# Moving runs of exponentials, and the attention steps behind them, inside a fused attention and feed-forward kernel

## The chip, the cores and the metric

The kernel runs on one core of a Trainium2 chip. The metric is the device time of one execution in microseconds (us); smaller is better. The engines that matter here are TensorE (PE in the rows), ScalarE (ACT), VectorE (DVE), GpSimd (POOL) and the queue of SyncE that issues transfers (SP). Each engine takes its own instructions in the order in which the program emits them, and waits at each for what that instruction needs.

## What is computed

An attention with a softmax of q over the head dimension and a softmax of k over the sequence, followed by a feed-forward layer with SiLU:

```python
q, k, v: (batch 8, heads 8, seq 576, head_dim 64)
q_s = softmax(q, axis=-1)                       # exp, row sums, divide
k_s = softmax(k, axis=2)
kv  = einsum('bhsd,bhse->bhde', k_s, v)
x   = einsum('bhsd,bhde->bhse', q_s, kv)        # then (4608 tokens, 512)
h   = x @ w_in                                  # 512 -> 2048
out = (h * sigmoid(h)) @ w_out                  # 2048 -> 512
```

## The kernel before

**Chunks.** The 4608 tokens are worked through in nine chunks t = 0 to 8 (chunk 0 has 576 columns, chunk 1 has 448, the others 512). For each chunk `mm1` (L202) makes 16 blocks of h: four matmuls into one PSUM bank, which ScalarE reads with SiLU into GT (L220). I write mm1(t, i) for the i-th block of chunk t. The second product of chunks 0 and 1 is plain: `mm2` (L324) has 16 steps of four matmuls. Step i = 4 qd + tb works on row block tb and needs the GT blocks 4 qd to 4 qd + 3; the rows for tb = 3 gather in a bank of the PSUM ring. Chunks 2 to 8 use a Strassen form instead: seven products 1, 6, 2, 7, 5, 4, 3 (`product`, L253), each in two halves a and b of eight matmuls of 256 columns, with sums of GT on VectorE before them (`presum`, L227: the S1, S2, S4 of L231, L233 and L237). Products 1 and 2 gather in the same bank A. When 1b is done, ScalarE copies the bank to s1 (L295); product 2 then adds onto that bank, so its first matmul may not start before this copy is done.

**Attention.** Batch b feeds chunk b (576 rows a batch against 512 a chunk, so that batch 7 feeds the last two). Its steps: transfers of q, k, v (L82); four exponentials of 128x1152 on ScalarE, two of q into eq, two of k into ek (L91); sums of eq and their reciprocals on VectorE (L105, L106); the multiplication by these on GpSimd (L111); a cast of v into vaug on GpSimd (L98); one transfer that transposes eq into qT (`tr_dma`, L122, on the SP queue); `kv` on TensorE in two halves (L153) and its scaling on VectorE (`kvcopy`, L165, L166); `xt` on TensorE in two halves (L187) and two copies on ScalarE for each (L198), which give the chunk its XT.

**Tables.** Exponential and SiLU need different tables on ScalarE. So a run of exponentials between SiLUs has a table load ahead of it (in the rows with L91) and one behind it (with L220). Plain copies need none.

**The ring.** Eight PSUM banks: three (`ops`) for the second product, five in a ring for mm1, `kv` (two banks for each half), `xt` (two for each half), and for one row block of mm2 of chunks 0 and 1. A new tile takes the bank of the ring that was given back longest ago in program order, and waits for the last reader of that bank.

**Order.** The program writes a list of units: the mm1 blocks of all chunks in order, and behind chosen mm1 blocks one step of mm2 or one half product (`trail`, L437). From chunk 3 on a chunk has 30 units: mm1(t, 0), (t, 1), (t, 2), then half products and mm1 blocks in turn: 1a, mm1(t, 3), 1b, mm1(t, 4), 6a, mm1(t, 5), 6b, mm1(t, 6), 2a, and so on to 3b; the half products are those of chunk t - 1. The steps of the attention are emitted ahead of a unit that is counted back from the first unit of their chunk (`plan_attn`, L459). A tuple (-34, -34) puts the exponentials of q and of k 34 units ahead; the next ones are for the casts of v, for the transposing transfer, for `kv` and for `xt`. Sums and multiplication of eq stand two and four units behind the exponentials of q, and the loads of the next batch one unit behind the transposing transfer and the casts.

The rest of the order is the same list read from front to back:

```python
    for u, (_, f) in enumerate(units):
        for g in at[u]:
            g()
        f()
```

Of the kernel before, what the change touches and what calls it, by code (L numbers as in the profile page):

```python
# [16 lines left out]
def kernel(  # L17
# [21 lines left out]
    NFB = DFF // 128  # L39
# [37 lines left out]
    def load(b, name, src, ccs=None, eng=nc.sync):  # L77
        if name not in st[b]:
            st[b][name] = ld.tile([128, NG, J * D], FP32, name=name, bufs=LDB[name])
        x = src[b].rearrange("(g r) (p j) d -> g (r p) (j d)", r=2, j=J).rearrange("g x y -> x g y")  # L80
        c = slice(0, NG) if ccs is None else slice(2 * ccs, 2 * ccs + 2)
        eng.dma_start(out=st[b][name][:, c, :], in_=x[:, c, :])  # L82
# [4 lines left out]
    def exp(b, src, dst, cc):  # L87
        if dst not in st[b]:
            st[b][dst] = ap.tile([128, J, NG * D], BF16, name=dst, bufs=1)
        o = st[b][dst][:, :, cc * 128:(cc + 1) * 128].rearrange("p j (g d) -> p j g d", d=D)  # L90
        nc.scalar.activation(out=o, in_=jgd(st[b][src], cc), func=ACT.Exp)  # L91

    def vcast(b, cc, eng):
        o = vaug[b % 2].rearrange("p j (g e) -> p j g e", e=E1)[:, :, 2 * cc:2 * cc + 2, 0:D]
        if eng is nc.scalar:
            eng.copy(out=o, in_=jgd(st[b]["vt"], cc))
        else:
            eng.tensor_copy(o, jgd(st[b]["vt"], cc))  # L98

    def qsum(b, cc):  # L100
        if "zq" not in st[b]:
            st[b]["zq"] = ap.tile([128, 2, J, 2], FP32, name="zq")
            st[b]["rzq"] = ap.tile([128, 2, J, 2], FP32, name="rzq")
        e = st[b]["eq"][:, :, cc * 128:(cc + 1) * 128].rearrange("p j (g d) -> p j g d", d=D)
        nc.vector.reduce_sum(out=st[b]["zq"][:, cc], in_=e, axis=AX.X)  # L105
        nc.vector.reciprocal(out=st[b]["rzq"][:, cc], in_=st[b]["zq"][:, cc])  # L106

    def qnorm(b, cc, eng):
        e = st[b]["eq"][:, :, cc * 128:(cc + 1) * 128].rearrange("p j (g d) -> p j g d", d=D)
        r = st[b]["rzq"][:, cc]  # L110
        eng.tensor_tensor(  # L111
            out=e, in0=e, in1=r[:, :, :, None].to_broadcast([128, J, 2, D]), op=ALU.mult
        )
# [7 lines left out]
    def tr_dma(b, eng):  # L121
        eng.dma_start_transpose(  # L122
            out=qt_tile(b).rearrange("x j c y -> x (j c) y"),
            in_=st[b]["eq"].rearrange("x j y -> x (j y)"),
        )
# [20 lines left out]
    def kv(b, cc):  # L146
        t = [ps.tile([128, 512], FP32, name="kvps", tag="ring", bufs=PSB["ring"]) for _ in range(2)]
        st[b]["kvps", cc] = t
        for j in range(J):
            for g in range(2):  # L150
                for r in range(2):
                    G = 2 * cc + g
                    nc.tensor.matmul(  # L153
                        out=t[r][g * 64:(g + 1) * 64, 0:E1],
                        lhsT=st[b]["ek"][r * P:(r + 1) * P, j, G * D:(G + 1) * D],
                        rhs=vaug[b % 2][r * P:(r + 1) * P, j, G * E1:(G + 1) * E1],
                        start=(j == 0),
                        stop=(j == J - 1),
                    )

    def kvcopy(b, cc):
        for r in range(2):
            kp = st[b]["kvps", cc][r]
            rz = ap.tile([128, 1], FP32, name="rz", bufs=4)
            nc.vector.reciprocal(out=rz, in_=kp[:, D:E1])  # L165
            nc.vector.tensor_scalar_mul(  # L166
                out=kvn[b % 3][:, cc, r, :], in0=kp[:, 0:D], scalar1=rz[:, 0:1]
            )
# [155 lines left out]
    def mm2(t, i):  # L324
        qd, tb = divmod(i, 4)
        if qd == 0:
            tag = "ops" if tb < 3 else "ring"
            OP[t, tb] = ps.tile([128, DM], FP32, name="ops", tag=tag, bufs=PSB[tag])
        n = NFB // 4
        for fc in range(qd * n, (qd + 1) * n):  # L330
            nc.tensor.matmul(  # L331
                out=OP[t, tb],
                lhsT=GT[t][:, fc, tb * 128:(tb + 1) * 128],
                rhs=W2[:, fc, :],
                start=(fc == 0),
                stop=(fc == NFB - 1),
            )
        if qd == 3:
            store(t, tb, tb % 2)

    def store(t, tb, dve=0):
        ost = mp.tile([128, DM], FP32, name="oq", bufs=4)
        if dve:
            nc.vector.tensor_scalar_mul(out=ost, in0=OP[t, tb], scalar1=1.0)
        else:
            nc.scalar.activation(out=ost, in_=OP[t, tb], func=ACT.Copy, scale=1.0)
        for i in range(2):
            b, col = divmod(t * TCH + tb * 128 + i * P, S)
            rows = out[b * S:(b + 1) * S, :].rearrange("(p j) o -> j p o", j=J)[col // P]
            nc.sync.dma_start(out=rows, in_=ost[i * P:(i + 1) * P, :])  # L350
# [86 lines left out]
    def trail(x, key, f):  # L437
        behind[min(max(x, 0), len(xs) - 1)].append((key, f))
# [1 line left out]
    for i in range(NFB):  # L440
        trail(min(5 + i, NFB - 1), ("mm2", 0), lambda i=i: mm2(0, i))
    for i in range(NFB):
        trail(NFB + 5 + i + max(i - 10, 0) * 3 // 2, ("mm2", 1), lambda i=i: mm2(1, i))
    for t in range(STD, NCH):
        for i, (m, a) in enumerate((m, a) for m in ORDER for a in range(2)):
            late = 3 if t == NCH - 2 and i > 6 else 0
# [5 lines left out]
    begin = {t: next(u for u, f in enumerate(units) if f[0] == ("mm1", t)) for t in range(NCH)}  # L452
# [3 lines left out]
    def plan(u, f):  # L456
        at[u].append(f)

    def plan_attn(b, u, sm, vs, tp, ks, ox, eng=nc.gpsimd):  # L459

        for i, (x, y) in enumerate((("qt", "eq"), ("kt", "ek"))):
            plan(u + sm[i], lambda x=x, y=y: [exp(b, x, y, cc) for cc in range(2)])
        for cc in range(2):
            plan(u + sm[0] + 2 + 2 * cc, lambda cc=cc: (qsum(b, cc), qnorm(b, cc, nc.gpsimd)))
            plan(u + vs[cc], lambda cc=cc: vcast(b, cc, eng))
        plan(u + tp, lambda: tr_dma(b, nc.sync))
        if b == 1:
            plan(u + vs[0] + 1, lambda: load_behind(2))  # L470
        elif b + 1 < B:
            plan(u + (tp - 5 if b == 2 else tp + 1), lambda: load(b + 1, "qt", q))
            plan(max(u + tp, u + max(vs)) + 1, lambda: [load(b + 1, *y) for y in (("kt", k), ("vt", v))])
        for cc in range(2):
            plan(u + ks[cc], lambda cc=cc: kv(b, cc))
            plan(u + ks[cc] + 1, lambda cc=cc: kvcopy(b, cc))
        for cc in range(2):
            plan(u + ox[cc], lambda cc=cc: xt(b, cc))

    def load_behind(b):  # L480

        st[b]["qt"] = ld.tile([128, NG, J * D], FP32, name="qt", bufs=LDB["qt"])
        nc.vector.tensor_copy(st[b]["qt"][0:1, 0, 0:1], vaug[(b - 1) % 2][0:1, J - 1, D:E1])
        for x in (("qt", q), ("kt", k), ("vt", v)):
            load(b, *x)

    V = nc.vector
    plan_attn(1, begin[1], (-18, -11), (-6, -5), -11, (-4, -3), (-2, 0), V)
    plan_attn(2, begin[2], (-21, -18), (-14, -13), -13, (-10, -7), (-5, -3))
    plan_attn(3, begin[3], (-25, -20), (-19, -16), -16, (-12, -9), (-6, -4))  # L490
    for b in range(4, B):
        plan_attn(b, begin[b], (-34, -34), (-32, -28), -23, (-14, -10), (-7, -4))
    for cc in range(2):
        plan(begin[NCH - 1] - 7 + 3 * cc, lambda cc=cc: xt(NCH - 1, cc))

# [44 lines left out]
```

## Time and profile before

| | us |
|---|---|
| median of 3 runs | 305.64 (305.04 to 305.79) |
| the profiled execution | 305.13 |
| its span, from the first to the last instruction | 303.3 |
| busy in that span: PE, ACT, DVE, POOL | 272.2, 178.7, 121.0, 53.9 |
| TensorE idle for ScalarE and VectorE, all waits together | 22.5 (the four rows of the group on TensorE's waits) |
| mean granted TensorE clock | 0.98 of full |

A row of a group or of the timeline names the line of the kernel, the engine, the operation, what it writes and reads, and the count; in brackets or behind a bar stands the idle time of the engine just before it and what ended that. Starts are given from the start of the span. Matmuls are pipelined, and the end that a row gives for a matmul is modelled: the next unit starts some 0.17 us before it.

### The profile page before, as it was taken

What the parts mean: (1) busy time and instruction counts of PE and PEld (TensorE: products, weight loads), DVE (VectorE), ACT (ScalarE), POOL (GpSimd) and SP (SyncE); (2) the same over time, 40 slices, a digit from 0 to 9 for tenths busy, and PEclk for the clock granted to TensorE, in tenths of its full rate; (3) what the DMA queues carried; (4) which work ended last, traced back from release to release, by engine and by line L of the source; (5) the groups of instructions that cost most, each with busy time, mean ns of one, the idle gap of its engine ahead of it and who ended that gap; (6) DMA issues with size and microseconds to landing.
All of it is one profiled execution on the core that took longest, in us unless ns stands there. A gap on an engine that the chain in (4) does not pass through costs nothing.

```text
span 303.3 us, 5523 instructions
## 1 busy us (share of the span) xinstructions
PE 272.2 (90%) x2306; PEld 163.3 (54%) x2306; DVE 121.0 (40%) x217; ACT 178.7 (59%) x287; POOL 53.9 (18%) x44
## 2 busy tenths in 40 slices
PE   8799789949789949999799969996999999999993
PEld 3466454414334316665466536654665665666882
DVE  3820425532305252435643474347443241423521
ACT  5694984892996983349744973488335445445110
POOL 0640310080160090002600170008000000000000
PEclk9999999997999968999999999999999999999999
DMA  7999999949149609811595149523212111201144
GB/s 264 270 198 282 325 237 347 317 132 301 53 85 382 219 10 287 284 37 43 107 360 168 46 99 335 198 55 83 47 30 64 37 35 37 69 0 38 40 100 104
DMA packets 42377, 46.43 MB, mean 153 GB/s; under 512 B 18544, under 2 KB 29808, under 8 KB 42352
## 3 DMA queue, kind: packets, MB, share of 16 engines
q1 hardware_dynamic: 37312, 38.35, 42.9%
q0 software_dynamic: 5040, 7.73, 11.5%
q8 instruction: 18, 0.29, 0.4%
q14 instruction: 7, 0.06, 0.1%
HBM read 36.70 MB, written 9.44 MB: 152 GB/s over the span
## 4 chain that ended last, share of the span: by engine, by line
PE 60%; ACT 22%; DMA 8%; DVE 4%; issue 3%; POOL 1%; SPq 0%; ACTq 0%
PE hps L206 27%; PE ops L273 25%; DMA qt<-in_q_dram 6%; ACT ek L91 5%; ACT L220 4%; ACT L91 4%; ACT eq L91 4%; PE ops L331 4%; ACT GT L220 3%; DMA vt<-in_v_dram 3%; DVE SW L231 2%; PE kvps L153 2%; ACT XT L198 2%; PE o L187 2%; DVE SW L233 2%
## 5 line engine op out<-in xcount | busy, mean ns | idle before, releaser
L206 PE MATMUL hps<-XT,W 128*128 128x512 bf16 (+3 forms) x640 | 146.1, 363 | 10.8 <-ACT GT L220 10.2
L220 ACT ACTIVATE GT<-hps 128x512 bf16<-128x512 f32 (+2 forms) x176 | 85.5, 526 | 86.9 <-PE hps L206 86.4
L206 PEld LDWEIGHTS <-W 128*128 128x128 bf16 x640 | 61.6, 99 | 62.0 <-issue 17.4
L273 PEld LDWEIGHTS <-GT 128*128 128x128 bf16 x448 | 43.8, 99 | 21.7 <-ACT GT L220 6.2
L111 POOL TENSOR_TENSOR eq<-eq,rzq 128x1152 bf16<-128x1152 bf16 x14 | 29.8, 2135 | 143.4 <-DVE rzq L106 143.4
L273 PEld LDWEIGHTS <-SW 128*128 128x128 bf16 x336 | 32.6, 98 | 14.5 <-DVE SW L233 3.5
L105 DVE TENSOR_REDUCE zq<-eq 128x18 f32<-128x1152 bf16 x16 | 21.4, 1339 | 41.4 <-ACT eq L91 41.4
L331 PE MATMUL ops<-W,GT 128*128 128x512 bf16 x128 | 33.7, 388 | 4.3 <-ACT GT L220 4.3
L273 PE MATMUL ops<-W,GT 128*128 128x256 bf16 x224 | 30.1, 278 | 5.3 <-ACT GT L220 5.3
L273 PE MATMUL ops<-TW,SW 128*128 128x256 bf16 x224 | 29.2, 273 | 2.7 <-DVE SW L233 2.7
L273 PE MATMUL ops<-TW,GT 128*128 128x256 bf16 x224 | 28.6, 273 | 0.0
L231 DVE TENSOR_TENSOR SW<-GT 128x1024 bf16<-128x1024 bf16 x14 | 14.5, 1032 | 23.9 <-ACT GT L220 23.9
L290 DVE SCALAR_TENSOR_TENSOR u<-ops,s 128x512 f32<-128x512 f32 x14 | 9.7, 692 | 34.9 <-PE ops L273 34.9
L198 ACT CAST XT<-o 128x512 bf16<-128x512 f32 (+3 forms) x36 | 18.3, 564 | 6.4 <-PE o L187 6.4
L331 PEld LDWEIGHTS <-GT 128*128 128x128 bf16 x128 | 12.2, 99 | 16.7 <-ACT GT L220 4.8
L91 ACT ACTIVATE eq<-qt 128x1152 bf16<-128x1152 f32 x16 | 17.8, 1156 | 2.7 <-DMA qt<-in_q_dram 2.6
L91 ACT ACTIVATE ek<-kt 128x1152 bf16<-128x1152 f32 x16 | 17.8, 1152 | 1.6 <-DMA kt<-in_k_dram 1.6
L290 DVE SCALAR_TENSOR_TENSOR oq<-ops,u 128x512 f32<-128x512 f32 x14 | 9.6, 687 | 17.3 <-PE ops L273 14.1
L98 POOL CAST vaug<-vt 128x1152 bf16<-128x1152 f32 x12 | 15.6, 1311 | 0.0
L220 ACT ACT_TABLE_LOAD x11 | 14.1, 1283 | 0.2
L273 PE MATMUL ops<-W,SW 128*128 128x256 bf16 x112 | 14.2, 273 | 0.0
L233 DVE TENSOR_TENSOR SW<-SW,GT 128x1024 bf16<-128x1024 bf16 x14 | 13.0, 930 | 0.5
(45 smaller groups left out, 136.9 us busy)
## 6 DMA issues: line engine op xcount, KB each, us to landing
qt<-in_q_dram SPq DMA_DIRECT2D x6, 1152.0 KB, 6.2
kt<-in_k_dram SPq DMA_DIRECT2D x6, 1152.0 KB, 8.6
vt<-in_v_dram SPq DMA_DIRECT2D x6, 1152.0 KB, 11.7
out_dram<-oq SPq DMA_DIRECT2D x42, 128.0 KB, 2.4
out_dram<-oq SPq DMA_DIRECT2D x60, 64.0 KB, 2.1
W<-in_moe_w_in_dram POOLq DMA_DIRECT2D x4, 512.0 KB, 9.6
W<-in_moe_w_out_dram POOLq DMA_DIRECT2D x4, 512.0 KB, 17.7
qt<-in_q_dram SPq DMA_DIRECT2D x2, 576.0 KB, 4.1
```

What stands on the lines that cost most here:

```text
L91: nc.scalar.activation(out=o, in_=jgd(st[b][src], cc), func=ACT.Exp)
L98: eng.tensor_copy(o, jgd(st[b]["vt"], cc))
L105: nc.vector.reduce_sum(out=st[b]["zq"][:, cc], in_=e, axis=AX.X)
L111: eng.tensor_tensor(out=e, in0=e, in1=r[:, :, :, None].to_broadcast([128, J, 2, D]), op=ALU.mult)
L198: nc.scalar.copy(out=x, in_=o1[g][:, 0:size])
L206: nc.tensor.matmul(out=hps[:, 0:size], lhsT=W1[:, c, fb * 128:(fb + 1) * 128], rhs=XT[t][:, c, off:off + size], start=(c == 0), stop=(c == ...
L220: nc.scalar.activation(out=GT[g][:, fb, col:col + n], in_=hps[:, h], func=ACT.Silu)
L231: V.tensor_add(S1[:, f], quad(t, 0, f, 1), quad(t, 1, f, 1))
L233: V.tensor_sub(S2[:, f], S1[:, f], quad(t, 0, f, 0))
L273: nc.tensor.matmul(out=o[:, a, :], lhsT=l(f), rhs=r(f), start=bool(first and a == 0 and f == 0), stop=(f == HF - 1), skip_group_check=True,)
L290: nc.vector.scalar_tensor_tensor(out=out, in0=o, scalar=1.0, in1=x, op0=ALU.mult, op1=ALU.add)
L331: nc.tensor.matmul(out=OP[t, tb], lhsT=GT[t][:, fc, tb * 128:(tb + 1) * 128], rhs=W2[:, fc, :], start=(fc == 0), stop=(fc == NFB - 1),)
```

## The change

It moves emission points and changes no instruction. The second-product steps of chunk 1 are spread over mm1 blocks 22 to 44 of the whole list (two for every three blocks) in place of blocks 21 to 31 one each and the last five over 33 to 43. The exponentials of batches 4 to 7 move from 34 to 25 units ahead of their chunk, and the steps behind them move later and closer together; batches 2 and 3 get new points of the same kind. Batch 1 and batch 0 stay as they are.

```diff
     for i in range(NFB):
-        trail(NFB + 5 + i + max(i - 10, 0) * 3 // 2, ("mm2", 1), lambda i=i: mm2(1, i))
+        trail(NFB + 6 + i * 3 // 2, ("mm2", 1), lambda i=i: mm2(1, i))
...
     plan_attn(1, begin[1], (-18, -11), (-6, -5), -11, (-4, -3), (-2, 0), V)
-    plan_attn(2, begin[2], (-21, -18), (-14, -13), -13, (-10, -7), (-5, -3))
-    plan_attn(3, begin[3], (-25, -20), (-19, -16), -16, (-12, -9), (-6, -4))
+    plan_attn(2, begin[2], (-16, -10), (-10, -9), -9, (-5, -4), (-3, -1))
+    plan_attn(3, begin[3], (-23, -17), (-17, -15), -15, (-10, -8), (-5, -3))
     for b in range(4, B):
-        plan_attn(b, begin[b], (-34, -34), (-32, -28), -23, (-14, -10), (-7, -4))
+        plan_attn(b, begin[b], (-25, -25), (-23, -21), -14, (-11, -9), (-5, -3))
```

Read off the list of units, the order around the exponentials is this. Before, those of batches 4 to 7 stand ahead of mm1(b-2, 12) for b = 4 and mm1(b-2, 14) for b = 5 to 7, so that the last SiLUs of that chunk come behind them; after, they stand ahead of the half product 1b in chunk b - 1, behind the SiLU of mm1(b-1, 3) and ahead of the copy s1 and the SiLU of mm1(b-1, 4). For batch 2 the exponentials of q stand ahead of mm2(1, 0) in both, with mm1(1, 6) moved in front of them, and those of k move from mm1(1, 7) to mm1(1, 10). For batch 3 they move from mm1(1, 14) and mm1(2, 1) to mm1(2, 1) and mm1(2, 5).

## Rows read from the trace of the kernel before

**Rows 1.** TensorE's waits: for whom, us in total, times, longest us.
```profile
PE hps L206 <- ACT GT L220: 10.2, 5, 4.3
PE ops L273 <- ACT GT L220: 5.3, 3, 1.8
PE ops L331 <- ACT GT L220: 4.3, 1, 4.3
PE ops L273 <- DVE SW L233: 2.7, 3, 0.9
```
**Rows 2.** Timeline of TensorE, chunks 1 and 2: start, us, instruction, [idle before].
```profile
56.11 1.03 PE L331 MATMUL ops<-W,GT 128*128 128x512 bf16 x4
...
60.97 1.03 PE L331 MATMUL ops<-W,GT 128*128 128x512 bf16 x4
...
62.59 0.81 PE L331 MATMUL ops<-W,GT 128*128 128x512 bf16 x3
67.68 0.39 PE L331 MATMUL ops<-W,GT 128*128 128x512 bf16 x1 [4.28 <-ACT GT L220]
...
83.27 2.21 PE L206 MATMUL hps<-XT,W 128*128 128x512 bf16 x8 [1.98 <-ACT GT L220]
...
90.73 1.89 PE L206 MATMUL hps<-XT,W 128*128 128x512 bf16 x8 [0.94 <-ACT GT L220]
92.55 0.48 PE L153 MATMUL kvps<-vaug,ek 64*64 64x65 bf16 x36
92.96 1.04 PE L331 MATMUL ops<-W,GT 128*128 128x512 bf16 x4
...
110.06 3.57 PE L206 MATMUL hps<-XT,W 128*128 128x512 bf16 x8 [4.28 <-ACT GT L220]
113.42 1.91 PE L273 MATMUL ops<-W,GT 128*128 128x256 bf16 x8
```
**Rows 3.** Stretches: us, busy PE, PEld, DVE, ACT, POOL, granted clock, DMA share, GB/s.
```profile
50.00:75.00 25.00, 20.50 (x163) 9.34 (x162) 9.90 (x20) 17.93 (x24) 6.65 (x4) 0.93 0.82 264
75.00:100.00 25.00, 21.96 (x188) 9.49 (x187) 8.26 (x20) 20.68 (x30) 6.39 (x4) 1.00 0.59 188
100.00:110.00 10.00, 5.77 (x33) 2.40 (x32) 3.79 (x5) 9.49 (x12) 3.18 (x3) 0.96 0.37 123
110.00:137.00 27.00, 26.95 (x238) 16.23 (x238) 10.82 (x20) 12.19 (x23) 3.67 (x3) 0.89 0.57 174
137.00:150.00 13.00, 10.33 (x67) 6.29 (x66) 7.88 (x9) 11.78 (x16) 6.85 (x4) 1.00 0.29 63
```
**Rows 4.** Timeline of all engines around the border of chunks 3 and 4.
```profile
137.78 1.28 ACT L91 ACT_TABLE_LOAD   x1
...
139.07 2.22 ACT L91 ACTIVATE eq<-qt 128x1152 bf16<-128x1152 f32 x2
...
141.19 2.20 ACT L91 ACTIVATE ek<-kt 128x1152 bf16<-128x1152 f32 x2
...
142.57 2.41 SPq L320 DMA_DIRECT2D out_dram<-oq  x4
...
144.71 3.05 ACT L220 ACTIVATE GT<-hps 128x512 bf16<-128x512 f32 x6
...
145.36 0.28 PE L273 MATMUL ops<-W,GT 128*128 128x256 bf16 x1 [1.77 <-ACT GT L220]
...
147.44 2.75 SPq L122 DMA_TRANSPOSE qT<-eq  x1
147.58 0.66 ACT L295 ACTIVATE s<-ops 128x512 f32<-128x512 f32 x1
...
149.57 0.61 PE L273 MATMUL ops<-TW,SW 128*128 128x256 bf16 x4 [0.90 <-DVE SW L233]
```
**Rows 5.** The transposing transfers, and a store beside loads (stretch 86 to 93).
```profile
DMA to landing us min/median/max: 4.6/6.2/6.7
out_dram<-oq SPq DMA_DIRECT2D x1, 128.0 KB, 10.3
```

## The prediction

> **What bounds the kernel now.** I read TensorE's waits first. Its rows come to 22.5 us of idle time, and nearly all of it hangs on SiLUs that ScalarE had not done or on sums that waited for such SiLUs [rows 1]. TensorE is therefore the engine whose time counts, and ScalarE sets it back only where it is away for a run of exponentials. The timeline of TensorE gives the places. In chunk 1 it stands still for 4.28 us: the step mm2(1, 4) needs the SiLU of mm1(1, 7), which lies behind both runs of batch 2. In chunk 2 it waits 1.98 and 0.94 us for banks of the ring (batch 3) and then 4.28 us, because the exponentials of batch 4 stand ahead of the SiLU of mm1(2, 12) and all five banks are full [rows 2]. At the next three borders it waits 1.77 us and 0.90 us each: a half product needs the last SiLUs of the chunk, and product 6 the sums made from them [rows 1, 4]. In all 11.48 + 3 x 2.67 = 19.5 us.
>
> The stretches show a second cost. The granted clock is 0.93 in 50 to 75 and 0.96 and 0.89 in 100 to 137 [rows 3]. At half clock that is 25 x 0.07 x 2 = 3.5 us behind the first wait of 4.28 us, and 10 x 0.04 x 2 + 27 x 0.11 x 2 = 6.7 us behind the second, some 0.9 us of which were idle. These cost 1.6 us and 2.9 us of work (half of the busy part of each). Stretches whose longest waits are 1.98 and 1.77 us keep full clock [rows 2 to 4].
>
> **The change part by part.** Nothing is added or removed: the number of runs, and so of table loads, is the same (two for each of batches 1 to 3, one for each later one). What counts is what TensorE can do while ScalarE is away.
>
> *Prices.* One step of mm2 and one mm1 of 448 columns take 62.59 - 60.97 = 1.62 us, split by columns 0.866 and 0.756 us; an mm1 of 512 columns or a half product (8 x 256) costs 0.866 as well [rows 2]. A half of `kv` takes 92.96 - 92.55 = 0.41 us [rows 2], a half of `xt` about as much. A run of four exponentials takes 143.39 - 137.78 = 5.61 us with the load ahead of it, the load behind it 1.3, one of two exponentials 1.29 + 2.2 + 1.3 = 4.8. Waiting SiLUs follow each other every 0.5 us, and s1 takes 0.66 [rows 4].
>
> *Chunks 1 and 2, batches 2 and 3.* I place the new order on the times of before, from 56.11, where mm1(1, 5) has ended. mm1(1, 6) now comes first; its SiLU ends at 57.6 and the exponentials of q hold ScalarE to 62.4. The SiLUs of mm1(1, 7) to (1, 9) end by 63.9, those of k hold it to 68.7, and the SiLU of mm1(1, 10) ends at 69.25. TensorE runs without a wait through mm2(1, 4), to 65.7: that step's GT block is ready at 63.0, so the wait of before is gone. What is late next is the ring. `kv` of batch 2 takes two banks; by the order in which they come free these are those of mm1(1, 9) and mm1(1, 10). It starts at 69.3 and waits 3.55 us. Its second half needs the bank of mm1(1, 13), just issued, and waits 0.8. In chunk 2 the exponentials of q hold ScalarE from 77.3 to 82.2 while four free banks and two mm2 steps cover all but 0.2 us. Those of k hold it from 84.3 to 89.1, and the first half of `kv` of batch 3 waits for the bank of mm1(2, 6), 1.4 us; the ring's next bank then waits some 0.5 us for `kvcopy`, which stands behind the sums S1, S2 on VectorE. Together 6.4 us by starts; a row counts each from the modelled end, 0.17 us later, so 5.5 us in the rows' terms.
> Before, this stretch took 113.42 - 56.11 = 57.3 us, of which 11.5 were waits and 1.6 + 1.6 lost to the clock (of the second low stretch only 110.06 to 113.42 lies in it) [rows 2, 3]; 42.6 us of work remain. After: 42.6 + 5.5 = 48.1. Gain 9.2 us, and 1.3 us for the half clock behind 113.42 that no longer follows: 10.5 us.
>
> *Chunks 3 to 6, batches 4 to 7.* Let T be the start of 1b. The SiLU of mm1(t, 3) ends at T + 0.8, the exponentials at T + 6.4. Behind them on ScalarE stands first s1, then the table load, then the SiLUs. s1 ends at T + 7.1. TensorE does 1b, mm1, 6a, mm1, 6b, mm1, six units, to T + 5.2, and then wants to add product 2 onto bank A, which s1 has not yet read. This wait is new: 1.9 us by starts, 1.75 in the rows' terms, with 2a and all of TensorE's later units queued behind it. The trace of before has no such wait, as s1 there comes early [rows 4]; nearest are the rows of 1.77 and 0.90 us. Its price lies between 0 and 1.9: it is made of single durations, so I take 1.75. The ring isn't the limit: mm1(t, 4) to (t, 8) fill it at about T + 10.6, when SiLUs have run since T + 8.4. At the borders nothing stands ahead of the last SiLUs any more, and S2 has seven units' time to be made, so 2.67 goes. Batch 4: a cost of 1.75 (its old wait is counted above). Batches 5 to 7: 3 x (2.67 - 1.75) = 2.8 gained.
>
> *What moves with them.* Sums, multiplications and casts keep their order among themselves; GpSimd is otherwise empty, VectorE's next due work at the new place is the sum u2, which waits for s1 anyway, and the bank that u2 frees is wanted at T + 10.6. Cover: about 3 us; without it product 7 would wait. The transposing transfer needed 147.44 - 137.78 = 9.7 us from the table load [rows 4], here T + 10.5. On SP it now stands behind the stores of product 2, which wait for their copy behind the caught-up SiLUs (T + 11.1) and issue four times 0.6 us [rows 4]: T + 13.6. It lands 4.6 to 6.7 us later [rows 5], T + 18.2 to 20.3. `xt` wants it twenty units, two `kv` halves and the wait after T: 17.3 + 0.8 + 1.9 = T + 20.0. So it costs 0 to 0.3 us, taken as 0, with no cover left. The loads behind it on SP keep their distance to the next run (18 units); stores of product 5 come behind them as before.
>
> *A rule on table loads.* By the rows, an exponential starts 0.01 us after the end of its table load [rows 4]. [...]
>
> **Sum.** 10.5 - 1.75 + 2.8 = 11.55 us. The profiled execution took 305.13, so 293.6; the median of the runs is 0.5 above it: 294.1.
>
> **The rivals.**
> - *The wait of 3.55 us for the ring costs the clock.* Both waits of 4.28 us did, those up to 1.98 did not [rows 2, 3]; 3.4 in the rows' terms lies nearer the first. Price 1.6 us: 295.7. [...]
> - *s1 doesn't hold product 2.* Then 4 x 1.75 = 7.0 us less, but `xt` comes at T + 18.1 and waits for the transposing transfer, landing up to 1.3 us sooner too as SP is freed sooner; 0 to 2 us of each 1.75 come back: 287 to 294. Against it: product 2 adds onto the very bank that s1 reads.
> - *The four new waits for s1 each cost the clock*, 1.6 us each: 300.5. Against it: 1.77 and 0.90 us at one border cost none [rows 3, 4].
> - *The ring binds more often in chunks 1 and 2* than my placing says, up to 5.5 us again: 294 to 299.6.
> - *Slower: the transposing transfer comes late for `xt`.* From 2.9 us in each of four chunks on ((305.64 - 294.1) / 4) it eats the whole gain, which is a landing 9.3 us after the issue. A store of 128 KB beside the loads took 10.3 [rows 5]; at that, 3.9 us in each: 309.7. Against it: none of the transposing transfers took more than 6.7 [rows 5].
> - *Nothing moves*, since the waits had another cause: 305.6. Against it: each wait's row ends with the SiLU or sum behind the exponentials.
>
> **How the numbers follow.** Forecast 294.1: 0.50 (292.5 to 295.2). Clock lost once: 0.20. s1 doesn't hold: 0.08. s1's waits cost the clock: 0.07. Ring binds more: 0.07. Late transposing transfer: 0.05. Nothing moves: 0.03. A measurement here can tell 0.3%, 0.9 us. Faster 0.92, same 0.03, slower 0.05. The range takes in the first two, the ring and half of the case without s1's wait: 289.5 to 299.5.
>
> **What would show it.** Right: no wait for SiLU at the borders of chunks 3 to 6; a wait of TensorE at L273 for the copy of L295, four times about 1.75 us; a wait of `kv` (L153) for SiLU of 3 to 3.5 us in chunk 1; full clock from 110 on; product 1a of chunk 2 near 104. Wrong: `xt` (L187) waiting for qT, or a clock under 1.00 in chunks 3 to 6. If the first wait is over 4 us, or the four are under 1, my placing of ScalarE's work was wrong.

## The result and the profile after

The changed kernel takes 293.56 us (median of 4 runs, 292.40 to 295.74) against 305.34 us for the kernel before (4 runs): a ratio of 0.9625, 95% interval 0.9558 to 0.9693, or 11.8 us less. A second series of 6 runs on one chip gave 293.39 us against 305.00, the same ratio with the interval 0.9594 to 0.9656. The forecast was 294.1 us, and its range 289.5 to 299.5.

The page of the profiled execution (292.62 us, span 290.7): busy time of TensorE and its clock in 40 slices.

```profile
PE 263.8 (91%) x2269; PEld 162.4 (56%) x2306; DVE 115.7 (40%) x217; ACT 178.0 (61%) x287; POOL 54.9 (19%) x44
...
PEclk9999999999999999999999999999999999999999
```

The two low places of the clock are gone in this execution; another execution of the same kernel shows two others (last experiment). Some matmul records are missing here (2269 of 2306), so the busy time is a little too low. TensorE's waits after the change, to be read against [rows 1] (us in total, times, longest):

```profile
PE ops L273 <- ACT s L295: 6.6, 4, 1.8
PE hps L206 <- ACT GT L220: 3.2, 2, 1.9
PE kvps L153 <- ACT GT L220: 2.8, 3, 1.9
PE kvps L153 <- ACT vaug L96: 2.1, 2, 1.1
PE kvps L153 <- POOL vaug L98: 1.4, 1, 1.4
```

Of [rows 1] only a 3.2 is left, in chunk 0, which the change doesn't touch. Everything at L273 for SiLU or sums and the wait at L331 are gone. New are four waits for s1, 6.6 us, and waits of `kv` of batches 2 and 3 for the ring (2.8) and for GpSimd's cast (1.4). Those for L96 stand in chunk 0, as before. The timeline of TensorE in chunks 1 and 2, against [rows 2]:

```profile
57.95 1.03 PE L331 MATMUL ops<-W,GT 128*128 128x512 bf16 x4
...
65.94 1.03 PE L331 MATMUL ops<-W,GT 128*128 128x512 bf16 x4
68.33 0.19 PE L153 MATMUL kvps<-vaug,ek 64*64 64x65 bf16 x1 [1.37 <-POOL vaug L98]
70.39 0.48 PE L153 MATMUL kvps<-vaug,ek 64*64 64x65 bf16 x35 [1.86 <-ACT GT L220]
70.82 0.92 PE L206 MATMUL hps<-XT,W 128*128 128x448 bf16 x4
71.67 0.48 PE L153 MATMUL kvps<-vaug,ek 64*64 64x65 bf16 x36
...
90.29 0.21 PE L153 MATMUL kvps<-vaug,ek 64*64 64x65 bf16 x1 [0.70 <-ACT GT L220]
90.77 0.48 PE L153 MATMUL kvps<-vaug,ek 64*64 64x65 bf16 x35 [0.27 <-ACT GT L220]
...
104.13 1.04 PE L273 MATMUL ops<-W,GT 128*128 128x256 bf16 x8
```

mm2(1, 4), for which TensorE stood still 4.28 us before, is the row at 65.94 and waits for nothing. `kv` of batch 2 waits 1.37 + 1.86 us instead. Product 1a of chunk 2 starts at 104.13 (113.42 before). The new place of the exponentials, in chunk 3, where the half product 1b starts at 105.86:

```profile
106.68 1.28 ACT L91 ACT_TABLE_LOAD   x1
...
107.97 2.22 ACT L91 ACTIVATE eq<-qt 128x1152 bf16<-128x1152 f32 x2
...
110.09 2.20 ACT L91 ACTIVATE ek<-kt 128x1152 bf16<-128x1152 f32 x2
...
112.20 0.58 ACT L295 ACTIVATE s<-ops 128x512 f32<-128x512 f32 x1
112.79 1.28 ACT L220 ACT_TABLE_LOAD   x1
...
112.83 1.03 PE L273 MATMUL ops<-W,GT 128*128 128x256 bf16 x8 [1.81 <-ACT s L295]
...
119.16 2.77 SPq L122 DMA_TRANSPOSE qT<-eq  x1
```

The copy s1 stands behind four exponentials, and product 2a starts 0.05 us after it has ended. No row of `xt` waits for qT.

### The profile page after: what moved, and what is told of

Same layout as the page of the kernel before. It is cut to its first block, busy times and chain, and to the rows that moved or that the text cites. A ratio compares the mean times of both kernels' runs of the same rounds, so it can differ in the third digit from the quotient of the medians.

```text
span 290.7 us, 5481 instructions
## 1 busy us (share of the span) xinstructions
PE 263.8 (91%) x2269; PEld 162.4 (56%) x2306; DVE 115.7 (40%) x217; ACT 178.0 (61%) x287; POOL 54.9 (19%) x44
## 4 chain that ended last, share of the span: by engine, by line
PE 54%; ACT 20%; DMA 18%; issue 3%; SPq 2%; POOL 2%; DVE 0%; ACTq 0%
PE ops L273 24%; PE hps L206 23%; DMA qt<-in_q_dram 8%; DMA out_dram<-oq 7%; ACT ek L91 5%; ACT L91 4%; ACT eq L91 4%; PE ops L331 3%; DMA vt<-in_v_dram 3%; ACT L220 3%; ACT GT L220 3%; PE kvps L153 2%; PE o L187 2%; SPq L122 1%; ACT s L295 1%
## 5 line engine op out<-in xcount | busy, mean ns | idle before, releaser
L206 PE MATMUL hps<-XT,W 128*128 128x512 bf16 (+3 forms) x612 | 139.2, 357 | 5.4 <-ACT GT L220 3.2
L206 PEld LDWEIGHTS <-W 128*128 128x128 bf16 x640 | 61.9, 98 | 52.4 <-issue 5.9
L273 PEld LDWEIGHTS <-GT 128*128 128x128 bf16 x448 | 43.4, 98 | 22.0 <-issue 8.5
L273 PEld LDWEIGHTS <-SW 128*128 128x128 bf16 x336 | 31.9, 98 | 9.4 <-issue 0.8
L273 PE MATMUL ops<-W,GT 128*128 128x256 bf16 x224 | 28.7, 272 | 6.6 <-ACT s L295 6.6
L331 PE MATMUL ops<-W,GT 128*128 128x512 bf16 x120 | 31.5, 379 | 0.6 <-issue 0.2
L273 PE MATMUL ops<-TW,GT 128*128 128x256 bf16 x224 | 28.6, 273 | 0.4
L273 PE MATMUL ops<-TW,SW 128*128 128x256 bf16 x224 | 28.8, 273 | 0.0
L231 DVE TENSOR_TENSOR SW<-GT 128x1024 bf16<-128x1024 bf16 x14 | 9.6, 689 | 27.1 <-ACT GT L220 27.1
L331 PEld LDWEIGHTS <-GT 128*128 128x128 bf16 x128 | 12.1, 98 | 12.1 <-issue 0.7
L273 PE MATMUL ops<-W,SW 128*128 128x256 bf16 x112 | 14.2, 273 | 0.0
L153 PE MATMUL kvps<-vaug,ek 64*64 64x65 bf16 x576 | 8.1, 194 | 6.4 <-ACT GT L220 2.8
## 6 DMA issues: line engine op xcount, KB each, us to landing
vt<-in_v_dram SPq DMA_DIRECT2D x6, 1152.0 KB, 11.8
```

The lines of the kernel that those rows point to most:

```text
L153: nc.tensor.matmul(out=t[r][g * 64:(g + 1) * 64, 0:E1], lhsT=st[b]["ek"][r * P:(r + 1) * P, j, G * D:(G + 1) * D], rhs=vaug[b % 2][r * P:( ...
L206: nc.tensor.matmul(out=hps[:, 0:size], lhsT=W1[:, c, fb * 128:(fb + 1) * 128], rhs=XT[t][:, c, off:off + size], start=(c == 0), stop=(c == ...
L231: V.tensor_add(S1[:, f], quad(t, 0, f, 1), quad(t, 1, f, 1))
L273: nc.tensor.matmul(out=o[:, a, :], lhsT=l(f), rhs=r(f), start=bool(first and a == 0 and f == 0), stop=(f == HF - 1), skip_group_check=True,)
L331: nc.tensor.matmul(out=OP[t, tb], lhsT=GT[t][:, fc, tb * 128:(tb + 1) * 128], rhs=W2[:, fc, :], start=(fc == 0), stop=(fc == NFB - 1),)
```

## The experiments

Each changes only points of emission and leaves out no work. Where times of different series are set against each other, the ratios to the kernel before of the same series are used.

**Which batches carry the gain: the late ones alone.**

```diff
-        plan_attn(b, begin[b], (-34, -34), (-32, -28), -23, (-14, -10), (-7, -4))
+        plan_attn(b, begin[b], (-25, -25), (-23, -21), -14, (-11, -9), (-5, -3))
```
(the rest as before)

> The kernel before with only the points of batches 4 to 7 moved. My theory: the wait of 4.28 us in chunk 2 and the 2.9 us of half clock behind it go, the borders lose 3 x 2.67 us, four waits for s1 of 1.65 us (as the changed kernel shows them) come: 4.28 + 2.9 + 8.0 - 6.6 = 8.6 us less than before, some 296.8 us. The first wait of 4.28 us in chunk 1 and its half clock stay. Rival: the spread of the steps of mm2 carries most of the gain; then this run stays above 301 us.

Measured 297.78 us against 305.26 before: 7.5 us less, 1.1 us short of the theory, far from the rival's 301. The profiled run (298.28 us) has two places of low clock, beside the last slice, that the profile of the kernel before doesn't have. One is behind a wait of 2.4 us in chunk 0, which the change doesn't touch. Of the 40 slices of the clock, in tenths of full, it is the sixth; the tenth is behind the first wait of 4.28 us, as before. Half clock, in the forecast and here, is what the profile of the kernel before shows at its two waits of 4.28 us: a granted clock of 0.50 over 68.5 to 71.5 and over 109.5 to 115.5, and 1.00 over 71.6 to 109 and over 116 to 137.

```profile
PE hps L206 <- ACT GT L220: 4.4, 2, 2.4
```
```profile
PEclk9999979997989999999999999999999999999998
```

The other, the twelfth slice, is behind batch 3's wait of 1.98 us. This wait is the same as before, but the eight matmuls behind it take 3.04 us, where [rows 2] have 2.21, and the stretch around them has a granted clock of 0.89 (us, busy PE, PEld, DVE, ACT, POOL, clock, DMA share, GB/s):

```profile
85.11 3.04 PE L206 MATMUL hps<-XT,W 128*128 128x512 bf16 x8 [1.98 <-ACT GT L220]
```
```profile
80.00:95.00 15.00, 12.90 (x62) 5.20 (x60) 3.10 (x4) 14.86 (x19) 6.39 (x4) 0.89 0.38 89
```

So the clock fell behind a wait of 1.98 us here and didn't before, where it is 1.00 over 80 to 86 and here 0.72 over 84 to 90. How much of the shortfall of the median each place makes isn't shown. The borders behave as forecast: four waits for s1, 6.4 us in all, and none for SiLU or sums.

**The early batches and the steps of mm2 alone.**

```diff
-        plan_attn(b, begin[b], (-25, -25), (-23, -21), -14, (-11, -9), (-5, -3))
+        plan_attn(b, begin[b], (-34, -34), (-32, -28), -23, (-14, -10), (-7, -4))
```
(from the changed kernel)

> The changed kernel with the old points for batches 4 to 7. My theory: the first wait of 4.28 us goes, but the exponentials of batch 4 again hold up chunk 2 by about 4 us with half clock behind it, and the borders of chunks 3 to 5 wait 1.77 + 0.90 us again: 8.6 us above the changed kernel, 302.2 us. Rival (the gain lies in chunks 1 and 2): below 297 us.

Measured 299.59 us, ratio 0.9812 (0.9776 to 0.9849): 5.7 us less than before, between the two. The borders wait again as in [rows 4]. What I had wrong was the price of batch 4: with the new order it holds up TensorE by 3.04 us, through the copies of `xt` that stand behind its exponentials, and not by 4.28, and no half clock follows (the clock of the stretch around it is 1.00):

```profile
106.28 1.89 PE L206 MATMUL hps<-XT,W 128*128 128x512 bf16 x8 [3.04 <-ACT XT L198]
```
```profile
90.00:115.00 25.00, 20.30 (x185) 10.09 (x183) 11.83 (x22) 20.31 (x31) 7.05 (x5) 1.00 0.77 230
```

The two parts bring 7.5 and 5.7 us singly, each to within some 1.1 us, and 11.8 together. Batch 4's wait is counted in both: it was 4.28 us before and is 3.04 and 0.51 us here. How much of the clock is counted twice isn't shown.

**The old places of the steps of mm2.**

```diff
-        trail(NFB + 6 + i * 3 // 2, ("mm2", 1), lambda i=i: mm2(1, i))
+        trail(NFB + 5 + i + max(i - 10, 0) * 3 // 2, ("mm2", 1), lambda i=i: mm2(1, i))
```

> The changed kernel with the old places of the second-product steps of chunk 1. My theory: the wait for GT in mm2(1, 4) stays away, since the exponentials of batch 2 then stand behind mm1(1, 7) anyway; kv of batch 2 waits some 2.6 us for its bank and mm1(2, 0) some 2 us for copies of xt that stand behind the exponentials of batch 3: 1 to 2 us above the changed kernel, 294 to 297 us. Rival (the spread of the steps is what removes the first wait): 4.28 us and the half clock come back, 299 us.

Measured 298.45 us (297.08 to 298.90), ratio 0.9774: nearly the rival's 299, though not by the rival's mechanism. No step of mm2 waits for GT. What comes is the wait of mm1(2, 0) for the copies of `xt` behind batch 3's exponentials, 3.27 us where I had 2, and half clock twice: the granted clock is 0.91 over 60 to 100, so 40 x 0.09 x 2 = 7 us at half.

```profile
82.64 2.78 PE L206 MATMUL hps<-XT,W 128*128 128x512 bf16 x6 [3.27 <-ACT XT L198]
```
```profile
60.00:100.00 40.00, 32.99 (x285) 14.57 (x284) 12.11 (x29) 31.40 (x40) 12.79 (x8) 0.91 0.48 135
```

This order costs some 4.5 us ((0.9774 - 0.9625) x 305), but that is not the price of the spread alone. The points of batches 2 and 3 are counted back from the first unit of their chunk, and with the old places four more steps of mm2 stand ahead of chunk 2, so the exponentials move as well. Those of batch 2 come to stand ahead of mm1(1, 8) and mm1(1, 11), so that mm1(1, 7), whose SiLU mm2(1, 4) needs, is ahead of them. Those of q of batch 3 come to stand ahead of mm1(1, 15) and of the second half of `xt` of batch 2; in the changed kernel they stand behind both halves. The 3.27 us follow from that place. What the spread is worth with the exponentials kept at their blocks of mm1 isn't shown.

**s1 ahead of the exponentials.** One unit later, and the copy comes first.

```diff
-        plan_attn(b, begin[b], (-25, -25), (-23, -21), -14, (-11, -9), (-5, -3))
+        plan_attn(b, begin[b], (-24, -24), (-23, -21), -14, (-11, -9), (-5, -3))
```

> The changed kernel with the exponentials of batches 4 to 7 one unit later, so that the copy s1 stands ahead of them on ScalarE. My theory: the four waits of product 2 for s1 (1.65 us each) go, and no wait for the ring takes their place, as mm1(t, 9) wants its bank when it has been free for 0.4 us; xt is wanted at 18.4 us after 1b, the transposing transfer lands 18.0 (at 4.6 us) to 20.1 (at 6.7 us): 287.0 us if all land in time, up to 291 with waits of xt or PEld at L187. Rival: the waits come from ScalarE's absence of 6.9 us as such, not from s1; then they stay in another place (L206 for SiLU) and the time stays at 293 to 294 us.

Measured 291.36 us, ratio 0.9539, 2.6 us less than the changed kernel and just above the top of the expected range. The waits for s1 are gone, and no wait for SiLU takes their place; half of the 6.6 us comes back as a wait for qT, the second limit named in the forecast:

```profile
PE o L187 <- DMA qT<-eq: 3.3, 4, 1.0
```
```profile
DMA to landing us min/median/max: 4.6/5.7/6.5
```

The transposing transfer is issued at 120.11 in chunk 3, right behind four stores of product 2 (117.61, 2.39 us for the four issues), and `xt` waits to 126.16. The transposing transfers also take longer: they land 5.7 us after their issue in the median, where the median of the changed kernel is 4.6. Why isn't shown.

**And the transposing transfer ahead of these stores.**

```diff
-        plan_attn(b, begin[b], (-24, -24), (-23, -21), -14, (-11, -9), (-5, -3))
+        plan_attn(b, begin[b], (-24, -24), (-23, -21), -17, (-11, -9), (-5, -3))
```

> As the run before it, and the transposing transfer and the loads behind it three units earlier, ahead of the stores of product 2 on SP. My theory: it is issued as soon as the multiplication on GpSimd is done, about 11.4 us after 1b, lands by 18.1 us at the latest, and no xt waits: 287.0 us. Rival (the transposing transfer was no limit): the same time as the run with s1 ahead within 0.5 us, and no wait at L187 in that one.

Measured 286.51 us, ratio 0.9398 (0.9361 to 0.9435). The transfer goes out at 118.49, the stores behind it. The median landing is 4.6 us after the issue again (4.6 to 5.5), and no row at L187 waits for qT any more:

```profile
118.49 2.69 SPq L122 DMA_TRANSPOSE qT<-eq  x1
121.28 3.17 SPq L320 DMA_DIRECT2D out_dram<-oq  x4
```

Against the changed kernel that is (0.9625 - 0.9398) x 305 = 6.9 us, the 6.6 us of its waits for s1. Both limits were real, and the second stood right behind the first.

**Batch 2 in one run.**

```diff
-    plan_attn(2, begin[2], (-16, -10), (-10, -9), -9, (-5, -4), (-3, -1))
+    plan_attn(2, begin[2], (-16, -16), (-10, -9), -9, (-5, -4), (-3, -1))
```
(from the changed kernel)

> The changed kernel with the four exponentials of batch 2 in one run (k at the place of q). My theory: one pair of table loads (2.6 us) goes from ScalarE; mm1(1, 11) waits 1.7 us for its bank, kv of batch 2 no longer waits (3.2 us before), nor does its half clock appear in any run: 1.7 us less in a run at full clock, and 0.8 us more on the median as the lost clock of about every other run goes: 291 to 292 us, mean granted clock over 0.99 in all runs. Rival (the lower clock has another cause than the wait of kv): runs with 0.984 stay, spread over 3 us as now.

Measured 290.40 us (289.90 to 290.62), ratio 0.9533, so (0.9625 - 0.9533) x 305 = 2.8 us less than the changed kernel, a little more than the 2.5 expected. The mean clock of its five runs is 0.997 to 0.999, the spread 0.7 us. One wait of 1.64 us is left, where 3.23 were, and `xt` of batch 2 waits 0.26 us for qT:

```profile
64.76 1.67 PE L206 MATMUL hps<-XT,W 128*128 128x448 bf16 x8 [1.64 <-ACT GT L220]
```

So the waits show 1.3 us of the 2.8. The rest goes with the clock, and not all of that need be batch 2's: these mean clocks leave no room for the low clock in the first 25 us either, which lies ahead of batch 2 and which the second profile of the changed kernel has (last experiment).

**kv of batch 2 a unit earlier**, so that it waits longer.

```diff
-    plan_attn(2, begin[2], (-16, -10), (-10, -9), -9, (-5, -4), (-3, -1))
+    plan_attn(2, begin[2], (-16, -10), (-10, -9), -9, (-6, -5), (-3, -1))
```

> The changed kernel with kv of batch 2 one unit earlier, ahead of mm2(1, 4): it waits for the same SiLU, so that the idle time grows by 0.87 us to about 4.1 us while the work stays the same. My theory: a wait of that length costs the clock in every run, as both of 4.28 us did before: all runs near 0.984, median 295 us, 1.5 us above the fast runs of the changed kernel. Rival: the clock depends on something else; then the runs spread as now, 292.4 to 295.7 us, half of them at full clock.

Measured 294.05 us, ratio 0.9666 (0.9632 to 0.9701). The wait is as long as planned (2.23 + 1.86 us), the clock over 60 to 80 is 0.83, so 20 x 0.17 x 2 = 6.8 us at half, and the mean clock is below 1 in all six runs (0.983 to 0.994).

```profile
66.75 0.19 PE L153 MATMUL kvps<-vaug,ek 64*64 64x65 bf16 x1 [2.23 <-POOL vaug L98]
68.80 0.71 PE L153 MATMUL kvps<-vaug,ek 64*64 64x65 bf16 x35 [1.86 <-ACT GT L220]
```

That doesn't tell the two theories apart: in the second series of the changed kernel (below) all six runs were below 1 as well, and the intervals of the two overlap. Inconclusive on how often; by the ratios the longer wait costs 1.3 us, which lies within the two intervals.

**Everything together**: the points (-24, -24) and -17 for batches 4 to 7, as with the transposing transfer ahead of the stores, and batch 2 in one run.

> s1 ahead of the exponentials, the earlier transposing transfer, and batch 2 in one run. My theory: the gains add, 6.6 + 1.7 + 0.8 us below the changed kernel: 284.5 to 285.5 us. Rival (TensorE falls into new waits once these go): above 287 us.

Measured 283.45 us (282.25 to 284.15), ratio 0.9300 (0.9267 to 0.9333): 7% below the kernel before, some 10 us below the changed one and 1 us under the expected range. The gains add within the intervals of about 1 us to either side: 0.9398 - 0.9300 is 3.0 us, against 2.8 for batch 2 alone.

**Batch 3 in one run too.**

```diff
-    plan_attn(3, begin[3], (-23, -17), (-17, -15), -15, (-10, -8), (-5, -3))
+    plan_attn(3, begin[3], (-23, -23), (-17, -15), -15, (-10, -8), (-5, -3))
```
(on top of the one before)

> The kernel with everything (s1 ahead, earlier transposing transfer, batch 2 in one run), and the exponentials of batch 3 in one run too (k at the place of q). My theory: a pair of table loads goes from ScalarE, but TensorE has only four free banks and two steps of mm2 to do meanwhile: mm1(2, 5) waits some 2.2 us for its bank, and the wait of kv of batch 3 (0.97 us) goes; 1.1 us slower than without, about 284.5 us beside 283.45. Rival (fewer table loads always pay here): 1 to 2.6 us faster, 281 to 282.5 us.

Measured 286.38 us, ratio 0.9352 (0.9308 to 0.9396), but in two groups: 283.25 and 283.62 us with a mean clock of 0.997, and four runs from 286.36 to 286.54 with 0.984 and 0.985. The wait is as placed, and in the profiled run half clock follows it: from start to start the three blocks of four matmuls behind it take 1.04, 1.71 and 1.53 us, where each takes 0.87 at full clock:

```profile
84.19 1.24 PE L206 MATMUL hps<-XT,W 128*128 128x512 bf16 x4 [2.19 <-ACT GT L220]
85.23 1.91 PE L331 MATMUL ops<-W,GT 128*128 128x512 bf16 x4
86.94 1.70 PE L206 MATMUL hps<-XT,W 128*128 128x512 bf16 x4
88.47 1.03 PE L331 MATMUL ops<-W,GT 128*128 128x512 bf16 x4
```

My term of 1.1 us was wrong: where the clock stays up, the run costs nothing against the kernel with everything (283.45 us); what makes the median worse is the clock, 3.0 us between the groups. Not all of that is batch 3's, for the profiled run has a second place of low clock, in the first 25 us, ahead of all that the edit moves:

```profile
0.00:25.00 25.00, 21.41 (x192) 12.01 (x195) 11.05 (x27) 16.36 (x31) 9.23 (x18) 0.93 1.02 244
```

The three blocks lose 4.28 - 3 x 0.87 = 1.7 us. In the first 25 us, 46 matmuls of L206 take 7.44 us, where they take 5.77 at full clock in the kernel before: another 1.7, so that both places make up the 3.0:

```profile
16.44 7.44 PE L206 MATMUL hps<-XT,W 128*128 128x320 bf16 x46 [0.29 <-DVE XT L196]
```
```profile
16.65 5.77 PE L206 MATMUL hps<-XT,W 128*128 128x320 bf16 x46 [0.28 <-DVE XT L196]
```

One run of exponentials in place of two, with one pair of table loads less, shortened the waiting in batch 2 (1.64 us for the ring in place of 3.23) and lengthened it in batch 3 (2.19 in place of 0.97): what counts is how much TensorE can do while ScalarE is away, and there the ring ends it 2.19 us too early.

**The changed kernel once more.**

> The changed kernel once more, for the spread of its times and of its clock, beside the other run on one chip. My theory: the half clock behind the wait of kv of batch 2 comes in some runs and not in others, and the time goes with it: runs at full clock near 292.5 us, runs with a mean clock of 0.984 to 0.994 up to 3 us slower. Rival: the time does not go with the mean clock.

Six runs, 292.76 to 294.72 us, mean clock 0.988 to 0.994: time and mean clock go together only in part (294.29 us at 0.994, 292.76 at 0.991). Two places of low clock are in its profiled run (294.72 us): one in the first 25 us, which the change doesn't touch, and one behind the wait of `kv`, which is again 1.37 + 1.87 us. The first run had the same wait and full clock. The stretch 60 to 85 of both, the first run first:

```profile
60.00:85.00 25.00, 21.43 (x180) 10.10 (x182) 7.81 (x16) 22.32 (x30) 9.14 (x6) 1.00 0.54 166
```
```profile
0.00:25.00 25.00, 20.64 (x187) 11.60 (x190) 11.05 (x27) 16.44 (x31) 10.46 (x18) 0.93 0.95 230
...
60.00:85.00 25.00, 21.32 (x174) 9.97 (x176) 7.09 (x15) 20.84 (x27) 7.01 (x5) 0.93 0.55 166
```

So the clock fell behind the same wait in one execution (0.93) and not in the other (1.00).

## Why the prediction was right, point by point

- **What bounds the kernel**: right. Taking ScalarE's runs off the places where TensorE has no cover removed the waits that the forecast named, and each part of the change removed its own (first two experiments). What the spread of the steps of mm2 does by itself isn't shown.
- **The sum**: forecast 294.1, median 293.56. That they lie so close is in part luck. The forecast holds no lost clock, and the run at full clock took 292.62, 1.5 us less; the two runs with a mean clock of 0.984 took 294.51 and 295.74 and lift the median.
- **Chunks 1 and 2**: forecast 57.3 to 48.1 us, a gain of 9.2. From the end of mm1(1, 5) (57.95 - 0.756 = 57.19) to 104.13 it took 46.9: 10.4. The waits were sized at 5.5 us in the rows' terms and are 1.37 + 1.86 + 0.70 + 0.27 and two of 0.16, 4.5. The first, for the bank of mm1(1, 10), was right (3.4 forecast, 3.2 measured), with GpSimd's cast ending some of it, which I hadn't counted. The second half of `kv` (0.8) didn't wait: it starts at 71.67, when the SiLU of mm1(1, 13) has not begun, so it took another bank than my list gave it. Which one, no row tells.
- **Chunk 0** took 1.1 us longer in this run (57.19 against 56.11), with a wait of 0.8 us for a transfer of W that [rows 1] do not have. The change doesn't touch it; it hides most of the 1.2 us by which the gain in chunks 1 and 2 was sized too small.
- **The waits for s1**: forecast 1.75 each, measured 1.81 and three times 1.59. Moving s1 ahead removed them, so the cause is shown. Right.
- **The borders** of chunks 3 to 6: no wait for SiLU or sums, right. From product 1a of chunk 2 to the end the span took 303.3 - 113.42 = 189.9 before and 290.7 - 104.13 = 186.6 after: 3.3 us, against 1.3 + 8.0 - 7.0 = 2.3 forecast. The cheaper waits for s1 are 0.4 of this 1.0; the rest has no row.
- **The transposing transfer**: forecast at 13.6 us behind 1b, measured 119.16 - 105.86 = 13.3; `xt` doesn't wait. "No cover left" was too strict: it took the slowest landing (6.7 us), and all four transfers landed after 4.6, in chunk 3 at 123.8, 2.3 us before `xt` starts at 126.11 (2.0 to 2.8 us in the four chunks). With the waits for s1 gone and the exponentials a unit later, qT is waited for four times.
- **The rival of the clock**: it is no rival but a part of the spread. The step that failed is the bound that I took from [rows 2, 3], that waits up to 1.98 us keep the clock: it fell behind a wait of 1.98 us in the first experiment (0.89 over 80 to 95), and behind one of 2.19 us in the profiled run with batch 3 in one run (0.94 over 60 to 90). One profile had shown one draw.
- **The table loads**: the forecast took from the rows that an exponential starts 0.01 us after its load has ended, and so it is here. The SiLU ahead of the load ends at 106.06 + 0.60 = 106.66, the load starts at 106.68 and ends at 107.96, and the exponential starts at 107.97.

## What to carry to other kernels

A long run on one engine belongs where the bounding engine has most work that doesn't need it, and what ends that cover can be counted from the order: the first bank that it still holds, the first block that it still owes, and the small copy that stands behind the run (here s1: one unit's shift was worth 2.6 us, and 6.9 once the next limit was moved too). When one such limit is removed, price the next one on the same path before the run: here it was a transfer behind four stores on its queue.

## What the runs showed of the hardware that was not expected

The granted clock of TensorE fell behind waits well under the 4.28 us of [rows 1], and behind the same wait in one execution and not in another. The low level is 0.50 of full in the kernel before (68.5 to 71.5 and 109.5 to 115.5). 1.98 us kept full clock in the profile of before and lost it in the first experiment, and 3.2 us went both ways in two profiled runs of the changed kernel. 2.19 us and 2.4 us lost it once each, and 3.04 us kept it in the second experiment. The four waits of 1.6 to 1.8 us for s1 left the clock at 1.00 in the stretches around them: 104 to 290 in the changed kernel and 85 to 280 in its second profile, 95 to 280 in the first experiment, 100 to 280 with batch 2 in one run.

The length of a single wait doesn't settle it either. In three profiles the clock of the first 25 us is 0.93: with everything together, with batch 3 in one run, and in the second of the changed kernel. The first two have a wait of 1.2 us ahead of the first matmul and waits of 1.0 us and less for the cast of v behind it; the kernel before has waits of 1.22 and 1.00 there too and kept 1.00. One such place costs some 1.7 us (rows of the experiment with batch 3 in one run). A difference of one or two us between medians of four to six runs can therefore be the draw of the clock and not the edit, so a profile is read for its low places before a gain is put down to a change.
